# The list of steps of a hand-scheduled attention and ELU kernel is written anew

## The chip, the cores and the metric

One core of one Trainium2 chip runs the whole program. The metric is the device time of one execution in microseconds (us). TensorE (PE) multiplies matrices, its weight loads are shown as an engine of their own (PEld), VectorE (DVE), ScalarE (ACT) and GpSimd (POOL) work on elements, and SyncE (SP) issues DMAs. ACT and POOL issue DMAs as well.

## The reference, cut to what matters

```
B, H, S, D = 8, 8, 576, 64;  factor = 4;  scale = 1/8
q_d, k_d, v_d = means of q, k, v over each 4 positions          # 144 positions
out_d     = softmax(scale * q_d @ k_d.T) @ v_d                  # coarse attention
out_local = softmax(scale * q @ k.T where |i-j| < 4) @ v        # a band of 7 keys
attn = repeat(out_d, 4) + out_local                             # [8, 8, 576, 64]
x = attn.transpose(0, 2, 1, 3).reshape(4608, 512)
h = x @ w_in                                                    # [4608, 2048]
g = where(h > 0, h, exp(min(h, 0)) - 1)                         # ELU
out = g @ w_out                                                 # [4608, 512], float32
```

## The kernel before, in words

**Attention.** A batch b has eight heads, taken as four pairs j. The scores of a pair are made transposed, in six windows of 96 queries against 112 keys, beside a coarse score of 144 by 144. Exponentials are taken without a maximum, the band is cut out by a mask, the sums of the exponentials come from matmuls with an indicator (constant IND), and their reciprocals are spread over partitions: by matmuls for b = 0 to 2, by a round trip through DRAM for b = 3 to 7.

**The two large products.** The tokens go in nine blocks t of 512. For each block, 16 groups fc of 128 hidden columns are made by four matmuls each (128x128 weights, 512 columns), pass through the ELU, and are then summed by 16 steps of four matmuls into four output tiles.

**One list sets every order.** Nothing is scheduled at run time. The string ORDER holds 1524 words, and the builder walks through it once; each engine gets its instructions in the order of the words that use it and executes them strictly in that order. What crosses engines is held by semaphores alone. The words that this document uses, with b the batch, j the pair, t the token block:

- `Lq b.j`, `Lk b.j`, `Lv b.j`: a load of float32 q, k or v of one pair, issued by SyncE (lines 306 and 316). From b = 3 the loads of q and k, and all loads of v, go in runs of 256 bytes. They land in ten buffers (tag f32). `Dq b.h`, `Dk b.h` (line 336): loads that cast, issued by POOL, two pairs at a time, for b = 1 and 2. `WL`: a one-element memset on POOL that keeps the next `Lv` from starting before POOL is there. `WI`, `WO`: quarters of the two weight matrices, issued by POOL.
- `Cq`, `Ck`, `Cv`: POOL's cast to float16, which frees the load's buffer.
- `Tq`, `Tk`: transposes on PE; `Aq`, `Ak`: ACT's copy out of PSUM; `Fq`, `Fk`, `KD`: sums of four on DVE; `VS`: coarse v on PE (from b = 3 within `Tq`), `VD` its copy out on DVE.
- `SC`: the scores of a pair on PE (for b = 0 in two parts, `SL`, `SD`); `E0`, `E1`: their exponentials on ACT, two instructions each; `M`: the mask on DVE; `DEN`, `RC`: the sums on PE and the reciprocals on DVE; `RB`: the spreading matmuls; `SO`, `SI`: the round trip, issued by ACT.
- `OUT`: the product with v on PE; `LG`: ACT's copy of it out of PSUM (b = 0 to 2); `MUL`: the division on DVE; `X b.j.t`: the sum of both attentions into the token block t, on POOL.
- `Q`, `mm1.t.fc`: the first product; `e`, `m`, `g`: exponential on ACT, minimum on DVE, and sum on DVE (into tile gt); `mm2.t.i`: a quarter of an output tile; `oc`: its copy out of PSUM on ACT; `st`: its store to DRAM, issued by ACT.
- `Zn`: n matmuls on constants put before the next use of the tag "two" in PSUM; `FILL`: nine of them at the start.

**PSUM.** From the first product on there are three pools of two slots: tag "two" (all of attention's tiles: a transpose, each head of a score, a product, a spread, a coarse v take one slot each), "hp" (first product) and "misc" (output tiles, sums, some of block 0's first product). A matmul that takes a slot waits for the engine that empties the slot's last tile.

**DMA completion.** The DMAs that SyncE and ACT issue share eight completion semaphores, dealt out in the order of the list, so a store or a round trip of ACT can be given the semaphore of an earlier load of SyncE. In the built program the later DMA is not issued before the earlier one on its semaphore has landed. In the list before, `st.0.0` waits in this way for `Lv2.1`, and `st.0.1` for `Lq3.0`.

**PE's tile shapes.** A matmul uses 128x128 of the array, or a part: 64x64 (`Tq`, `Tk` for b below 3), 64x128 (`SC`), 128x64 (`OUT`), 128x32 (`DEN`), 32x128 (`RB`).

Of the kernel before, what the change touches and what calls it, by code (L numbers as in the profile page):

```python
# [29 lines left out]
RW = RG * RN  # L30
# [18 lines left out]
Tk1.0 Aq1.0 m.0.3 m.0.1 Ak1.0 g.0.1 WO3 SC1.1 Fq1.0 WLv2.0 Dq2.0 Lv2.0 mm1.0.7 Fk1.0 E01.1 Lv2.1
Cv1.0 Lv2.2 g.0.3 E11.1 Lv2.3 g.0.2 VS1.0 Lq3.0 mm1.0.11 VD1.0 e.0.7 M1.1 mm1.0.13 e.0.6 m.0.7  # L50
e.0.11 g.0.7 SC1.0 m.0.6 e.0.13 mm1.0.5 m.0.11 g.0.11 E01.0 m.0.13 mm1.0.9 E11.0 g.0.13 g.0.6
Tq1.2 Tk1.2 M1.0 Aq1.2 mm1.0.14 Ak1.2 Lk3.0 Cv1.1 Fq1.2 OUT1.0 e.0.5 Fk1.2 mm1.0.4 e.0.9 m.0.5
LG1.0 g.0.5 Tq1.3 e.0.4 Dq2.1 m.0.9 VS1.1 g.0.9 Aq1.3 mm2.0.0 VD1.1 e.0.14 Fq1.3 Tk1.3 OUT1.1
Ak1.3 Dk2.1 m.0.4 g.0.4 LG1.1 Fk1.3 SC1.2 m.0.14 g.0.14 mm2.0.1 E01.2 mm1.0.12 E11.2 mm1.0.8
e.0.12 M1.2 SC1.3 Lv3.0 m.0.12 e.0.8 g.0.12 Cv1.2 E01.3 m.0.8 mm1.0.10 g.0.8 E11.3 VS1.2 e.0.10
mm1.0.15 M1.3 VD1.2 DEN1 e.0.15 m.0.10 g.0.10 OUT1.2 m.0.15 mm2.0.2 RC1 LG1.2 g.0.15 RB1.1 RB1.0
MUL1.1 mm2.0.3 MUL1.0 X1.1.1 RB1.2 oc.0.0 MUL1.2 X1.0.2 mm2.0.4 X1.1.2 X1.0.1 Tq2.1 st.0.0 Tk2.1
Aq2.1 Cv1.3 mm2.0.5 Ak2.1 Fq2.1 X1.2.1 VS1.3 Fk2.1 Tq2.2 X1.2.2 mm2.0.6 Aq2.2 VD1.3 OUT1.3 Fq2.2
RB1.3 LG1.3 mm2.0.7 MUL1.3 Tk2.2 oc.0.1 mm2.0.8 Cv2.0 Lq3.1 Ak2.2 mm2.0.9 X1.3.2 Fk2.2 X1.3.1
mm2.0.10 st.0.1 Cv2.1 mm2.0.11 VS2.0 oc.0.2 mm2.0.12 Cv2.2 Lk3.1 VD2.0 SC2.1 mm2.0.13 E02.1  # L60
# [124 lines left out]
def kernel(  # L185
# [92 lines left out]
    def nines(b):  # L278
        return b in NINES
# [481 lines left out]
```

## Time and profile before

| what | value |
|---|---|
| median of 6 runs | 365.6 us (364.04 to 368.89) |
| the profiled execution | 365.09 us, of which the span of its instructions is 363.3 us |
| granted TensorE clock, mean | 0.995 |
| PE busy | 348.5 us, 3953 matmuls |
| of these, first product and second product | 142.8 us and 139.8 us, 576 matmuls each |
| DVE, ACT, POOL busy | 240.3, 208.3, 120.3 us |
| DMA | 46.08 MB; 92314 of 106917 packets under 512 bytes |

The span runs from the first instruction to the last; 1.8 us of the execution lie outside it. In the trace a line such as L679 is a line of the kernel before. A matmul's end is modelled, so that matmuls that run one after the other overlap a little in the rows; the starts are what one counts with. "Idle before" is the time that the engine stood still ahead of a row, with what ended it. SPq and ACTq are the queues on which SyncE and ACT issue DMAs: a row there lasts from the start of the issue to its end, not to the landing.

### The profile page before, as it was taken

How to read it: one execution, taken by the hardware profiler on the slowest of the kernel's cores; microseconds unless marked ns; L12 is line 12 of the kernel's file. 1: busy time of each engine (PE TensorE's matmuls, PEld its weight loads, DVE VectorE, ACT ScalarE, POOL GpSimd, SP SyncE). 2: the span in 40 equal slices, each digit the busy share in tenths (PEclk: the TensorE clock that was granted, in tenths of full speed). 3: DMA queues.
4: the chain of work that ended last, by engine and by line, in shares of the span. 5: the costliest groups of instructions: out<-in, count | busy, mean ns of one | idle time of the engine just before them, and what ended most of it. 6: DMA issues, size and time to landing. Idle time of an engine off the chain costs nothing.

```text
span 363.3 us, 9507 instructions
## 1 busy us (share of the span) xinstructions
PE 348.5 (96%) x3953; PEld 183.0 (50%) x3953; DVE 240.3 (66%) x472; ACT 208.3 (57%) x395; POOL 120.3 (33%) x177
## 2 busy tenths in 40 slices
PE   7888989899999999999999999999999999999995
PEld 3564455545565564564555445554544544444442
DVE  2767986459888548587887677878565655455520
ACT  2855883478578759377466666776454334344321
POOL 6858224551474140850472218311400410000000
PEclk9899999999999999999999999999999999999999
DMA  8999999999879789499469942022004100010012
GB/s 269 222 203 200 200 197 196 201 175 197 155 149 208 117 181 167 101 213 190 113 114 195 203 75 69 32 83 60 31 33 112 56 34 30 29 60 29 29 60 87
DMA packets 106917, 46.08 MB, mean 127 GB/s; under 512 B 92314, under 2 KB 101178, under 8 KB 106874
## 3 DMA queue, kind: packets, MB, share of 16 engines
q1 hardware_dynamic: 91402, 25.17, 41.0%
q10 hardware_dynamic: 8896, 13.36, 12.6%
q0 software_dynamic: 6576, 6.94, 11.1%
q8 instruction: 31, 0.51, 0.6%
q14 instruction: 12, 0.10, 0.1%
HBM read 42.49 MB, written 9.53 MB: 143 GB/s over the span
## 4 chain that ended last, share of the span: by engine, by line
PE 78%; ACT 6%; DVE 4%; DMA 4%; issue 3%; SPq 2%; ACTq 1%; POOL 1%; POOLq 0%
PE op L679 32%; PE hp L635 28%; DMA v<-in_v_dram 4%; PE sc L476 3%; PE lg L584 3%; DVE gt L669 2%; PE den L539 2%; SPq L316 2%; ACT e L660 2%; PE tq L369 1%; PE tq L392 1%; PE tk L392 1%; PE tq L251 1%; ACT pex L502 1%; DVE e L664 1%
## 5 line engine op out<-in xcount | busy, mean ns | idle before, releaser
L635 PE MATMUL hp<-xt,WI 128*128 128x512 f16 x576 | 142.8, 379 | 2.2 <-DVE gt L669 2.0
L679 PE MATMUL op<-WO,gt 128*128 128x512 f16 x576 | 139.8, 380 | 0.4 <-DVE gt L669 0.3
L660 ACT ACTIVATE e<-hp 128x512 f16<-128x512 f32 x144 | 85.7, 601 | 74.3 <-PE hp L635 67.1
L669 DVE SCALAR_TENSOR_TENSOR gt<-hp,e 128x512 f16<-128x512 f32 x144 | 99.2, 690 | 4.7
L679 PEld LDWEIGHTS <-gt 128*128 128x128 f16 x576 | 53.2, 98 | 62.0 <-DVE gt L669 1.6
L635 PEld LDWEIGHTS <-WI 128*128 128x128 f16 x576 | 53.0, 97 | 60.8 <-issue 3.7
L664 DVE TENSOR_SCALAR e<-e 128x512 f16<-128x512 f16 x144 | 51.9, 362 | 47.9 <-ACT e L660 47.0
L627 POOL TENSOR_TENSOR xt<-ln,gn 128x64 f16<-128x64 f16 (+7 forms) x63 | 41.7, 684 | 66.8 <-DVE ln L614 66.4
L502 ACT ACTIVATE pex<-sc 112x576 f16<-112x576 f32 x64 | 40.9, 646 | 6.6 <-PE sc L486 4.2
L686 ACT COPY os<-op 128x512 f32<-128x512 f32 x36 | 21.1, 586 | 40.1 <-PE op L679 39.9
L359 POOL CAST v<-v 112x768 f16<-112x768 f32 x30 | 24.9, 842 | 37.2 <-PE lg L584 22.6
L521 DVE TENSOR_TENSOR mex<-pex,MASK 112x1152 f16<-112x1152 f16 x32 | 25.5, 797 | 13.2 <-ACT pex L502 13.1
L354 POOL CAST q<-q 96x768 f16<-96x768 f32 x20 | 16.8, 840 | 31.1 <-issue 21.3
L354 POOL CAST k<-k 96x768 f16<-96x768 f32 x20 | 17.3, 873 | 27.2 <-PE tk L392 20.6
L508 ACT ACTIVATE dex<-sc 72x288 f16<-72x288 f32 x64 | 25.4, 403 | 0.9 <-PE sc L486 0.9
L417 ACT CAST qt<-tq 128x720 f16<-128x720 f32 x20 | 15.2, 760 | 11.4 <-PE tq L369 7.9
L476 PEld LDWEIGHTS <-kt 64*112 64x112 f16 x384 | 13.3, 129 | 14.0 <-issue 10.1
L476 PE MATMUL sc<-qt,kt 64*112 64x96 f16 x384 | 17.2, 220 | 2.1 <-ACT kt L412 0.6
L369 PEld LDWEIGHTS <-VR 112*72 112x72 f16 x192 | 13.3, 115 | 5.8 <-ACT qt L412 2.2
L614 DVE TENSOR_TENSOR ln<-lg,rcb 128x576 f16<-128x576 f32 x20 | 15.0, 749 | 0.0
L450 DVE CAST vd<-tq 72x256 f16<-72x256 f32 x20 | 8.3, 414 | 8.8 <-ACT qt L417 8.7
L584 PEld LDWEIGHTS <-v 112*64 112x64 f16 x384 | 10.2, 109 | 7.4 <-issue 5.3
(64 smaller groups left out, 273.7 us busy)
## 6 DMA issues: line engine op xcount, KB each, us to landing
v<-in_v_dram SPq DMA_DIRECT2D x28, 336.0 KB, 7.5
out_dram<-os ACTq DMA_DIRECT2D x36, 256.0 KB, 2.8
q<-in_q_dram SPq DMA_DIRECT2D x24, 288.0 KB, 5.2
k<-in_k_dram SPq DMA_DIRECT2D x24, 288.0 KB, 6.1
rcb<-rd ACTq DMA_DIRECT2D x10, 360.0 KB, 5.4
WI<-in_moe_w_in_dram POOLq DMA_DIRECT2D x4, 512.0 KB, 11.6
WO<-in_moe_w_out_dram POOLq DMA_DIRECT2D x4, 512.0 KB, 16.4
q<-in_q_dram POOLq DMA_DIRECT2D x4, 288.0 KB, 11.5
```

The lines of the kernel that those rows point to most:

```text
L354: nc.gpsimd.tensor_copy(out=t, in_=x.rearrange("p (e c d) -> p c e d", e=2, d=D))
L359: nc.gpsimd.tensor_copy(out=t[:], in_=st32.pop(("v", b, j)).rearrange("p (e c) d -> p c e d", e=2))
L476: nc.tensor.matmul(sc[e][0:KW, c // 3, QB * (c % 3) : QB * (c % 3) + QB], kt[r, QB * c : QB * c + KW], q_of(b, j, r, c), start=True, stop= ...
L502: nc.scalar.activation(out=stS[(b, j)][2][:, e, :].rearrange("p (g u) -> p g u", g=2), in_=scs[(b, j)][e][0:KW, :, 0:HB], func=AF.Exp, sca ...
L508: nc.scalar.activation(out=stS[(b, j)][1][:, e], in_=scs[(b, j)][e][0:KG, :, HB : HB + SD], func=AF.Exp, scale=SCALE / 16.0,)
L521: nc.vector.tensor_tensor(out=mex[:], in0=pex[:], in1=mk2, op=AB.mult)
L627: eng.tensor_tensor(out=xts[t][:, j, t0 - TBLK * t : t1 - TBLK * t], in0=ln[:, a:z], in1=_rep4(gn[:, a // 4 : z // 4]), op=AB.add,)
L635: nc.tensor.matmul(hps[(t, fc)][:], WI[:, dc, 128 * fc : 128 * fc + 128], xts[t][:, dc, :], start=(dc == 0), stop=(dc == DMC - 1),)
L660: nc.scalar.activation(out=e[:], in_=hps[(t, fc)][:], func=AF.Exp)
L664: nc.vector.tensor_scalar(out=e[:], in0=e[:], scalar1=1.0, scalar2=-1.0, op0=AB.min, op1=AB.add)
L669: nc.vector.scalar_tensor_tensor(out=gts[t][:, fc, :], in0=hps[(t, fc)][:], scalar=0.0, op0=AB.max, in1=els.pop((t, fc))[:], op1=AB.add,)
L679: nc.tensor.matmul(ops[(t, tt)][:], gts[t][:, fc, 128 * tt : 128 * tt + 128], WO[:, fc, :], start=(fc == 0), stop=(fc == FCN - 1),)
```

## The change

The list is replaced. The new one holds the same 1524 words, each once more, in another order; the first 29 us of PE's work (to `Q2`) keep PE's, ACT's and DVE's order, and the order of SyncE's loads is the same throughout. Three things in the code go with it:

- the tile of `LG` (tag lg32) becomes one tile of twice the width for each two pairs, two buffers instead of four, so `LG` of pair 0 must come before that of pair 1, and 2 before 3;
- IND has 104 columns instead of 52 (the built load moves 112x104 instead of 112x52 elements);
- `load_v4`, `V4` and `STORE_SP` are added and not used: V4 is empty and STORE_SP is False, and no word of the list calls `U` or `V`.

From `X0.2.1` to `X1.3.1` (about 28 to 70 us of the profile before) the two lists read as follows.

```
-X0.2.1 X0.2.0 Q1 X0.3.0 Dk1.1 Q2 Dq1.1 mm1.0.0 mm1.0.2 e.0.0 X0.3.1 Tq1.1 WO0 Tk1.1 e.0.2 m.0.0
-mm1.0.1 g.0.0 Ak1.1 WO1 mm1.0.3 Aq1.1 m.0.2 mm1.0.6 Fk1.1 WO2 e.0.3 Fq1.1 e.0.1 Tq1.0 Dk2.0
-Tk1.0 Aq1.0 m.0.3 m.0.1 Ak1.0 g.0.1 WO3 SC1.1 Fq1.0 WLv2.0 Dq2.0 Lv2.0 mm1.0.7 Fk1.0 E01.1 Lv2.1
-Cv1.0 Lv2.2 g.0.3 E11.1 Lv2.3 g.0.2 VS1.0 Lq3.0 mm1.0.11 VD1.0 e.0.7 M1.1 mm1.0.13 e.0.6 m.0.7
-e.0.11 g.0.7 SC1.0 m.0.6 e.0.13 mm1.0.5 m.0.11 g.0.11 E01.0 m.0.13 mm1.0.9 E11.0 g.0.13 g.0.6
-Tq1.2 Tk1.2 M1.0 Aq1.2 mm1.0.14 Ak1.2 Lk3.0 Cv1.1 Fq1.2 OUT1.0 e.0.5 Fk1.2 mm1.0.4 e.0.9 m.0.5
-LG1.0 g.0.5 Tq1.3 e.0.4 Dq2.1 m.0.9 VS1.1 g.0.9 Aq1.3 mm2.0.0 VD1.1 e.0.14 Fq1.3 Tk1.3 OUT1.1
-Ak1.3 Dk2.1 m.0.4 g.0.4 LG1.1 Fk1.3 SC1.2 m.0.14 g.0.14 mm2.0.1 E01.2 mm1.0.12 E11.2 mm1.0.8
-e.0.12 M1.2 SC1.3 Lv3.0 m.0.12 e.0.8 g.0.12 Cv1.2 E01.3 m.0.8 mm1.0.10 g.0.8 E11.3 VS1.2 e.0.10
-mm1.0.15 M1.3 VD1.2 DEN1 e.0.15 m.0.10 g.0.10 OUT1.2 m.0.15 mm2.0.2 RC1 LG1.2 g.0.15 RB1.1 RB1.0
-MUL1.1 mm2.0.3 MUL1.0 X1.1.1 RB1.2 oc.0.0 MUL1.2 X1.0.2 mm2.0.4 X1.1.2 X1.0.1 Tq2.1 st.0.0 Tk2.1
-Aq2.1 Cv1.3 mm2.0.5 Ak2.1 Fq2.1 X1.2.1 VS1.3 Fk2.1 Tq2.2 X1.2.2 mm2.0.6 Aq2.2 VD1.3 OUT1.3 Fq2.2
-RB1.3 LG1.3 mm2.0.7 MUL1.3 Tk2.2 oc.0.1 mm2.0.8 Cv2.0 Lq3.1 Ak2.2 mm2.0.9 X1.3.2 Fk2.2 X1.3.1
-mm2.0.10 st.0.1 Cv2.1 mm2.0.11 VS2.0 oc.0.2 mm2.0.12 Cv2.2 Lk3.1 VD2.0 SC2.1 mm2.0.13 E02.1
...
+X0.2.1 X0.2.0 Q1 X0.3.0 X0.3.1 Dk1.1 Q2 Dq1.1 mm1.0.0 Tq1.1 e.0.0 mm1.0.2 WO0 Aq1.1 Tk1.1 m.0.0
+mm1.0.1 g.0.0 WO1 e.0.2 mm1.0.3 Tq1.0 Ak1.1 Fq1.1 Dk2.0 mm1.0.6 Aq1.0 m.0.2 Fk1.1 WO2 e.0.3
+Tk1.0 e.0.6 Fq1.0 Lv1.3 Cv1.0 Ak1.0 g.0.2 WO3 VS1.0 m.0.6 e.0.1 mm1.0.8 g.0.6 WLv2.0 Dq2.1 VD1.0
+mm1.0.4 m.0.1 g.0.1 SC1.1 Fk1.0 mm1.0.7 E01.1 m.0.3 g.0.3 E11.1 mm1.0.9 e.0.4 M1.1 SC1.0 e.0.7
+m.0.4 e.0.8 g.0.4 E01.0 m.0.8 g.0.8 e.0.9 Tq1.3 m.0.7 E11.0 mm1.0.10 m.0.9 g.0.9 Dq2.0 Aq1.3
+Tq1.2 M1.0 Lv2.0 mm1.0.13 Aq1.2 Fq1.3 Cv1.1 Tk1.2 Fq1.2 VS1.1 Ak1.2 g.0.7 Tk1.3 Fk1.2 e.0.10
+mm1.0.11 Dk2.1 VD1.1 Ak1.3 m.0.10 e.0.13 OUT1.0 g.0.10 e.0.11 mm1.0.5 Fk1.3 LG1.0 m.0.11
+mm1.0.15 g.0.11 e.0.5 m.0.13 SC1.2 g.0.13 mm2.0.0 E01.2 m.0.5 g.0.5 mm1.0.12 e.0.15 E11.2 m.0.15
+mm2.0.1 g.0.15 e.0.12 M1.2 SC1.3 Lv2.1 mm1.0.14 m.0.12 E01.3 g.0.12 Cv1.2 E11.3 OUT1.1 mm2.0.2
+e.0.14 M1.3 LG1.1 m.0.14 VS1.2 g.0.14 DEN1 VD1.2 OUT1.2 RC1 LG1.2 RB1.2 mm2.0.3 MUL1.2 RB1.1
+oc.0.0 X1.2.1 RB1.0 st.0.0 mm2.0.4 MUL1.0 X1.2.2 mm2.0.5 MUL1.1 X1.0.2 X1.0.1 mm2.0.6 Lv2.2
+X1.1.1 Tq2.1 Tk2.1 Aq2.1 Cv1.3 mm2.0.7 Ak2.1 Fq2.1 X1.1.2 Tq2.2 oc.0.1 Fk2.1 VS1.3 Aq2.2 mm2.0.8
+VD1.3 st.0.1 Fq2.2 OUT1.3 RB1.3 Cv2.0 Lv2.3 LG1.3 mm2.0.9 MUL1.3 Tk2.2 mm2.0.10 Ak2.2 X1.3.2
+X1.3.1 Fk2.2 VS2.0 Lq3.0 Tq2.0 VD2.0 Cv2.1 mm2.0.11 Aq2.0 Fq2.0 mm2.0.12 oc.0.2 Cv2.2 Lk3.0
```

The rest of the code:

```
 X_DVE, K_DVE = ((0, 3, 0),), ((0, 0), (0, 1))
+V4, STORE_SP = (), False
...
@@ -157,9 +158,10 @@
     vr = np.zeros((KW, 120), dtype=np.float16)
     for i in range(QB):
         vr[PAD + i, 48 + i // 4] = 0.25
-    ind = np.zeros((KW, 52), dtype=np.float16)
+    ind = np.zeros((KW, 104), dtype=np.float16)
     ind[:, 19] = 1.0
     ind[:, 39:51] = 1.0
+    ind[:, 52:104] = 4.0 * ind[:, 0:52]
     sel = np.zeros((NPAIR, 32, RN, 2, 64), dtype=np.float16)
     for e in range(2):
         for g in range(RN):
@@ -270,7 +272,7 @@
         src = moe_w_out.rearrange("(c p) m -> p c m", p=128)[:, n, :]
         nc.gpsimd.dma_start(out=WO[:, n, :], in_=src)
 
-    st32, st16, stV, stT, stS, stR = {}, {}, {}, {}, {}, {}
+    st32, st16, stV, stT, stS, stR, st4 = {}, {}, {}, {}, {}, {}, {}
     tp, scs, dens, rbs, lgs, lg32, lns, rcbs = {}, {}, {}, {}, {}, {}, {}, {}
     xts, gts, ops, hps, els, oss = {}, {}, {}, {}, {}, {}
     kts = {}
@@ -342,6 +344,25 @@
         )
         for i in range(2):
             st16[(n, b, 2 * h + i)] = t[:, i]
+
+    def wide():
+        return sb.tile([128, 2 * RW], FP32, tag="lg32", bufs=2, name="lg32")
+
+    def load_v4(h, b, i):
+        if not h:
+            t = wide()[0:KG, 0:1024].rearrange("p (g h d) -> p g h d", h=2, d=D)
+            for n in range(2):
+                st4[(b, 2 * i + n)] = t[:, 4 * n : 4 * n + 4]
+            st4[(b, i, "all")] = t
+        a = v[b, 4 * i]
+        nc.gpsimd.dma_start(
+            out=st4[(b, i, "all")],
+            in_=bass.AP(
+                tensor=a.tensor, offset=a.offset + 2 * D * h,
+                ap=[[4 * D, KG], [4 * D * KG, 8], [D, 2], [1, D]],
+            ),
+            **({"accum_op": AB.add} if h else {}),
+        )
 
     def cast_qk(n, b, j):
         t = sb.tile([128, 768], FP16, tag=n + "16", bufs=2, name=n + "16")
@@ -393,7 +414,7 @@
                 to[:, c // 3, QW * (c % 3) : QW * (c % 3) + QW], x[:, c, :, :],
                 at_once("I16")[:], start=True, stop=True,
             )
-        if n == "q":
+        if n == "q" and b not in V4:
             vsum_mm(b, j, to[:, :, GW : GW + 128])
 
     def away(n, b, j):
@@ -445,6 +466,12 @@
         vsum_mm(b, j, x)
 
     def v_away(b, j):
+        if b in V4:
+            vd = sb.tile([KG, 4, D], FP16, tag="vd", bufs=7, name="vd")
+            x = st4.pop((b, j))
+            nc.vector.tensor_tensor(out=vd[:], in0=x[:, :, 0], in1=x[:, :, 1], op=AB.add)
+            stV[(b, j)][1] = vd
+            return
         x = tp[("v", b, j)] if nines(b) else tp[("q", b, j)][:, :, GW : GW + 128]
         vd = sb.tile([KG, 2, 128], FP16, tag="vd", bufs=7, name="vd")
         nc.vector.tensor_copy(out=vd[:], in_=x[0:KG])
@@ -527,7 +554,8 @@
         for e in range(2):
             for g in range(RN):
                 r = RN * e + g
-                st = at_once("IND")[:, 19 - r : 51 - r]
+                o = 52 if b in V4 and g >= 8 else 0
+                st = at_once("IND")[:, o + 19 - r : o + 51 - r]
                 for kg in range(1 if g < 8 else 2):
                     for j in range(NPAIR):
                         mex, dex, _ = stS[(b, j)]
@@ -589,13 +617,15 @@
             for e in range(2):
                 nc.tensor.matmul(
                     lg[64 * e : 64 * e + 64, 0, HB : HB + SD],
-                    vd[:, kg, 64 * e : 64 * e + 64], dex[:, e, kg, :],
+                    vd[:, 2 * e + kg] if b in V4 else vd[:, kg, 64 * e : 64 * e + 64], dex[:, e, kg, :],
                     start=(kg == 0), stop=(kg == 1),
                 )
 
     def out_away(b, j):
         lg = lgs[(b, j)]
-        t = lg32[(b, j)] = sb.tile([128, RW], FP32, tag="lg32", bufs=4, name="lg32")
+        if j % 2 == 0:
+            lg32[(b, j // 2, 0)] = wide()
+        t = lg32[(b, j)] = lg32[(b, j // 2, 0)][:, RW * (j % 2) : RW * (j % 2) + RW]
         nc.scalar.copy(
             out=t[:, 0:S].rearrange("p (g u) -> p g u", g=2), in_=lg[:, :, 0:HB]
         )
@@ -687,7 +717,8 @@
 
     def store(t, tt):
         r = TBLK * t + 128 * tt
-        nc.scalar.dma_start(out=out[r : r + 128, :], in_=oss.pop((t, tt))[:])
+        eng = nc.sync if STORE_SP else nc.scalar
+        eng.dma_start(out=out[r : r + 128, :], in_=oss.pop((t, tt))[:])
 
     def first_fill():
         tp[("q", 0, 0)] = two("tq")
@@ -711,6 +742,8 @@
         does["T" + n] = lambda b, j, n=n: turn(n, b, j)
         does["A" + n] = lambda b, j, n=n: away(n, b, j)
         does["F" + n] = lambda b, j, n=n: fours(n, b, j)
+    does["U"] = lambda b, j: load_v4(0, b, j)
+    does["V"] = lambda b, j: load_v4(1, b, j)
     for i in range(2):
         does[f"E{i}"] = lambda b, j, i=i: exp_both(i, b, j)
         does[f"G{i}"] = lambda b, j, i=i: exp_local(i, b, j)
```

## The prediction

> **What bounds the kernel now.** I read the page's busy shares first, then PE's slices.
>
> ```profile
> PE 348.5 (96%) x3953; PEld 183.0 (50%) x3953; DVE 240.3 (66%) x472; ACT 208.3 (57%) x395; POOL 120.3 (33%) x177
> ...
> PE   7888989899999999999999999999999999999995
> ...
> ACT  2855883478578759377466666776454334344321
> ```
>
> PE is the bound, and as the same 3953 matmuls run in any order, a new list can win only the holes between them. The first eight slices (9 us each) hold most of the holes, so I cut the span by stage.
>
> ```profile
> core 0: us, PE busy (x) PEld busy (x) DVE busy (x) ACT busy (x) POOL busy (x), PEclk, DMA share, GB/s
> 0.00:27.90 27.90, 23.50 (x458) 14.66 (x459) 15.69 (x26) 15.15 (x31) 18.81 (x38) 0.94 1.11 230
> 27.90:64.50 36.60, 31.86 (x526) 17.22 (x524) 28.52 (x58) 23.61 (x49) 16.22 (x25) 1.00 1.20 198
> 64.50:95.00 30.50, 29.62 (x452) 16.25 (x453) 20.98 (x40) 20.55 (x41) 9.74 (x13) 1.00 1.17 193
> 95.00:300.00 205.00, 203.99 (x2249) 108.51 (x2248) 148.51 (x294) 126.34 (x238) 75.54 (x102) 1.00 0.58 115
> 300.00:359.70 59.70, 59.54 (x274) 26.38 (x272) 26.56 (x56) 22.08 (x39) 0.00 (x0) 1.00 0.12 45
> ```
>
> Columns: stretch, its length, busy time of each engine, granted clock. The DMA engines are full to 95 us. I then laid the list's words on the PE rows, start to start, and took for each kind of block its shortest distance as its work. Work is 339.0 us; 22.8 us are lost: about 9 before `mm1.0.0` at 30.49, 4.2 from there to 62, 2.0 in one hole at 62 to 65, 3.8 from 65 on, 3.8 behind PE's last block. The rest of the hole's story is in the chain that ended last.
>
> ```profile
> 49.02 14.32 DMA v<-in_v_dram
> ...
> 63.42 0.38 ACTq L690
> ...
> 63.84 0.65 ACT qt L412
> ...
> 64.53 0.53 PE vs L369 x6
> ```
>
> `Lv2.1` was 14.3 us under way. The store `st.0.0` could not be issued before (shared completion semaphore), so ACT stood; `Aq2.1` behind it came at 63.84, `VS1.3` (which needs its slot) at 64.53 instead of 62.66: 1.87 us.
>
> **The change part by part.** Every duration is from this one execution, 365.09 us (span 363.3 and 1.8 outside); it lies 0.5 under the median, so I sum against 365.09 and shift the result by 0.5.
>
> *To `mm1.0.0`:* PE, ACT and DVE keep their order. POOL swaps `WI` and `Dk1.0`, `Dq1.0`, all issues of some 0.75 us, with consumers far behind. Nothing; without that cover, one issue's 0.75 us. IND doubles to 22.8 KB of a 46 MB program: nothing. The paired lg32 buffers cost nothing, as DVE's `MUL` of one batch ends long before `LG` of the next; uncovered, `LG` waits one division, 0.75 us.
>
> *30.49 to `VS1.3`.* I stepped the new list through with these rows: a group of four matmuls 0.863 us (0.957 before another tile shape), `SC` 0.566, `OUT` 0.505, `e` 0.55 start to start on ACT, an exponential pair 0.83, an ACT copy 0.52, `m` 0.36, `g` 0.69, a cast 0.84 and an issue 0.75 on POOL. Two resources give waits: ACT behind exponentials and POOL behind issues. One in full: from the start of `SC1.1` PE needs 0.566 + 0.863 + 0.957 + 0.72 (a wait of `mm1.0.9` for `g.0.3`) + 0.566 = 3.67 us to `Tq1.3`, which takes the slot that `E01.0` empties. ACT starts 0.73 + 0.07 after `SC1.1`, does two pairs (1.66), `e.0.4`, `e.0.7`, `e.0.8` (1.64), then `E01.0` (0.83), ready at 4.95: a wait of 1.3. Queued behind the waiting `Tq1.3` is all of PE. The others, found so: `VS1.0` 0.9 (its cast stands behind POOL's issues, as it did before with 1.0), `mm1.0.8` 0.44, `mm1.0.9` 0.72, `RB1.2` 0.35 (reciprocals), `VS1.1` 0.25, `Tk1.3`, `OUT1.1` 0.17 each, `mm1.0.4` 0.1. Sum 4.45 against 4.19 before (0.55, 0.49, 0.49, 1.01, 0.14, 0.30, 0.68, 0.38, 0.15): **+0.3**.
>
> The row for such waits in the kernel before:
>
> ```profile
> 34.85 0.20 PE L476 MATMUL sc<-qt,kt 64*112 64x96 f16 x1 [0.45 <-ACT qt L412]
> 35.39 0.46 PE L476 MATMUL sc<-qt,kt 64*112 64x96 f16 x11 [0.34 <-ACT kt L412]
> ...
> 37.78 0.49 PE L369 MATMUL vs<-v,VR 112*72 112x128 f16 x6 [0.83 <-ACT dex L508]
> ```
>
> The last is named for ACT; POOL's cast of that v ended at 37.72, and it is what ended the wait.
>
> *The store wait.* SyncE's loads keep their order and, under full DMA engines, I let them land as before: `Lv2.1` 63.35, `Lq3.0` 69.08 (issued 61.96).
>
> ```profile
> v<-in_v_dram SPq DMA_DIRECT2D x1, 336.0 KB, 14.3
> ...
> q<-in_q_dram SPq DMA_DIRECT2D x1, 288.0 KB, 7.1
> ```
>
> In the new list three more quarters of `mm2` lie ahead of `Tq2.1`, so PE comes there at about 63.9 and `st.0.0` holds nobody. But `st.0.1`, tied to `Lq3.0`, is moved forward past `LG1.3` (before, it stood at `mm2.0.10`, issued 69.16 with nothing urgent behind). ACT now stands at it until 69.1; 0.38 for the issue and 0.81 for `LG1.3` end at 70.4, and `Tk2.2` waits for that slot. PE's work up to `Tk2.2` is 55.64 us in the new list; with 8.94 lost before `mm1.0.0` and 4.45 since, PE would be there at 69.0. The wait is 1.4, against 1.87 + 0.11 that disappear: **−0.6**. The stall is moved, not removed. Behind it on ACT are `Ak2.2`, `Aq2.0`, the first `e.1`. Unknown is the landing: by the two rows above the load takes 7.1 or 14.3 us; I take 7.1, the row of the same load. At the page's median for q, 5.2, it lands at 67.2 and costs nothing.
>
> The Trainium skill, page "DMA: Bandwidth & Descriptors", section "Anatomy of one DMA — SWDGE (gpsimd) path", fits a load's time as 2.0 us plus its bytes at 436 GB/s, for loads that POOL issues. That speaks against my wait: by it 288 KB are an estimated 2.7 us, `Lq3.0` lands near 64.7, and the sum would be 1.4 lower. The rows of 7.1 and 14.3 us for loads on SyncE's queue decide; this case does not show such speed while the queue is full.
>
> *Changes of tile shape.* Counted in built order PE changes shape 172 times before and 175 after.
>
> ```profile
> 141.60 1.89 PE L635 MATMUL hp<-xt,WI 128*128 128x512 f16 x8
> 143.42 0.51 PE L476 MATMUL sc<-qt,kt 64*112 64x96 f16 x12
> ```
>
> Eight matmuls at 0.216 are 1.73; the score starts 1.82 after: 0.09 for the change. Three more: **+0.3**.
>
> *65 us to the end.* Before, ten waits make 3.3 of the 3.8 us, nearly all for `g` (an hp slot is needed again too soon).
>
> ```profile
> L635 PE MATMUL hp<-xt,WI 128*128 128x512 f16 x576 | 142.8, 379 | 2.2 <-DVE gt L669 2.0
> L679 PE MATMUL op<-WO,gt 128*128 128x512 f16 x576 | 139.8, 380 | 0.4 <-DVE gt L669 0.3
> ```
>
> By the rows a slot comes free some 1.9 us after its last matmul (`e`, `g` in sequence); a gap of 1.52 filled with other PE work gave 0.38. In the new list such gaps are wide enough at `mm1.2.11`, `mm2.2.2`, `mm1.3.11`, `mm1.4.5`, `mm1.8.3`, `mm2.8.3` (0.38, 0.38, 0.31, 0.25, 0.18, 0.43): −1.9. New tight ones are `mm1.1.3` (gap 1.52: 0.4), `mm1.2.9` (1.75: 0.15), `VS2.1` (0.23) and `RB2.0` (0.1): +0.9. **−1.0**. Bounds: all 3.8 but the 0.9 and a last 0.2 go, −2.7; nothing is gained and the denser ACT work at 90 to 120 us (27 us of work in 30 instead of 23) costs 1.5, +1.5. I take −1.0, nearest to the counted gaps.
>
> Sum: 0 + 0.3 − 0.6 + 0.3 − 1.0 = −1.0. 365.09 becomes 364.1, the median **364.6**. It is no change that can be measured: 1%, 3.7 us, is about what a measurement of this kernel tells from none.
>
> **The rivals.**
>
> R1, faster. `Lq3.0` lands by 67.8 (the median of 5.2 us for q speaks for it, full DMA engines against), `st.0.1` costs nothing, and the 2.8 us of later waits vanish too, as the large holes past 65 us are few. 364.6 − 1.3 − 2.8 = 360.5.
>
> R2, slower. `st.0.1` is moved ahead of `LG1.3` and its load is late like `Lv2.1`: 14.3 us from 61.96 is 76.3, 7.2 later than 69.08, and ACT with PE behind it stands so much longer: 364.6 + 7.2 = 371.8. It decides, slower by over 1% (369.3), from a landing at 73.8 on. For it: loads of v before it took that long, and POOL's issues of WO and the casting loads compete on the same engines. Against: the loads issued from 56 to 66 us took 6 to 9 us.
>
> R3, the change does not do what it says: 172 shape changes become 175 and SyncE's order is the same, so a count of shapes wins nothing, and only those 0.3 us remain: 365.9.
>
> **How the numbers follow.** Forecast 0.55, R1 0.20, R2 0.20, R3 0.05. Faster by over 1% (under 361.9) is R1 and a little of the forecast, 0.21; slower is R2 and 0.04 of the forecast, 0.24; the rest 0.55. The range goes from R1's 360.5 to 370.5: what is left out is half of R2 and the end of R1. The forecast's own range is its two open terms, −1.3 (load) − 1.7 (later waits) to +2.5 (later waits): 361.6 to 367.1.
>
> **What would show it.** Right: no hole at 62, a wait of ACT of more than 1 us ended by a q load at 67 to 70, `Tk2.2` near 70.4, a 1.3 us wait at `Tq1.3` near 42, under 3 us of PE waits past 71, 3.8 us at the end. Wrong: an ACT wait at `st.0.1` past 73 or none; PE waits of several us for casts between 33 and 60; new waits for `g` past 90 us that sum to over 4.

## The result, and the profile after

| | before | after |
|---|---|---|
| median of the runs measured together | 366.44 us (70 runs) | 370.68 us (33 runs, 365.83 to 373.44) |
| ratio | | 1.0076, interval 1.0056 to 1.0096 |
| the profiled execution, and its span | 365.09, 363.3 us | 369.86, 368.1 us |
| mean granted clock over the span of the profiled execution | 0.995 | 0.986 |
| PE lost, as the prediction counts it: before `mm1.0.0` / to `Tk2.2` / to the last block | 8.9 / 6.1 / 3.9 us | 10.2 / 8.3 / 4.9 us |

It is slower, by 0.8%; 1.0 us less was forecast. The ratio is smaller than that of the medians (1.0116) because the comparison leaves out the runs that lie more than 1.5% above a kernel's fastest, which for the changed kernel are ten runs with a low granted clock; where the fastest of few runs was itself short of the full clock (e3 and e4 below), none is left out.

First four of the five stretches that were shown before the change: length, busy time of each engine, granted clock, DMA share. From 300 us on PE does not stand.

```profile
core 0: us, PE busy (x) PEld busy (x) DVE busy (x) ACT busy (x) POOL busy (x), PEclk, DMA share, GB/s
0.00:27.90 27.90, 23.04 (x442) 14.26 (x443) 14.76 (x24) 14.66 (x30) 17.60 (x36) 0.94 1.11 230
27.90:64.50 36.60, 31.51 (x477) 17.16 (x475) 27.99 (x53) 22.26 (x48) 12.97 (x20) 0.91 1.20 200
64.50:95.00 30.50, 29.80 (x383) 15.84 (x383) 20.49 (x39) 19.05 (x40) 15.04 (x20) 1.00 1.08 205
95.00:300.00 205.00, 202.85 (x2371) 109.15 (x2366) 149.29 (x297) 127.62 (x239) 75.05 (x102) 1.00 0.55 112
```

From 27.9 to 64.5 us PE is about as busy as before (31.5 against 31.9 us) but does 49 matmuls fewer, and the granted clock is 0.91 where it was 1.00. That column had no term in the prediction. From 95 to 300 us PE stands 1.1 us longer. PE's waits, by what ended them (total, times, longest):

```profile
PE vs L390 <- POOL v L380: 2.6, 1, 2.6
PE tq L407 <- ACT dex L535: 1.7, 1, 1.7
...
PE sc L503 <- DVE vd L477: 0.9, 1, 0.9
...
PE op L709 <- DVE gt L699: 0.7, 1, 0.7
```

The first two stand in the first product of block 0. They are `VS1.0` and `Tq1.3` on PE's timeline:

```profile
35.11 0.47 PE L407 MATMUL tk<-EYE,k 64*64 64x64 f16 x18
38.23 0.80 PE L390 MATMUL vs<-v,VR 112*72 112x128 f16 x6 [2.65 <-POOL v L380]
38.82 3.05 PE L665 MATMUL hp<-xt,WI 128*128 128x512 f16 x8
41.80 0.51 PE L503 MATMUL sc<-qt,kt 64*112 64x96 f16 x12
...
46.58 0.47 PE L407 MATMUL tq<-EYE,q 64*64 64x64 f16 x18 [1.70 <-ACT dex L535]
```

Eight matmuls of the first product take 1.82 us elsewhere, from their start to that of the score behind them; behind the first hole they take 2.98 (38.82 to 41.80). POOL's timeline tells why `VS1.0` is so late:

```profile
35.89 0.70 POOL L338 DMA_DIRECT2D k<-in_k_dram  x1 [1.61 <-PE tk L407]
36.58 0.77 POOL L273 DMA_DIRECT2D WO<-in_moe_w_out_dram  x1
37.34 0.84 POOL L380 CAST v<-held 112x768 f16<-112x768 f32 x1
```

`Dk2.0` reuses a buffer that `Tk1.0` reads, so POOL stands until PE has done `Tk1.0`; then come two issues and the cast `Cv1.0`, 2.3 us in a row. The new list has `VS1.0` on PE right behind `Tk1.0`, so all of that chain is PE's wait. Before, `SC1.1` and `mm1.0.7` stood between: 1.4 us of work and a wait of 0.5.

The clock is best read on its own grid. Cut into pieces of 3.41 us that begin where its steps are:

```profile
34.32:37.74 3.42, 1.26 (x22) 0.66 (x21) 3.38 (x7) 2.75 (x6) 1.85 (x3) 1.00 1.30 198
37.74:41.15 3.41, 2.92 (x12) 1.47 (x12) 2.51 (x6) 0.00 (x0) 1.83 (x4) 0.50 1.21 197
41.15:44.56 3.41, 3.41 (x40) 1.63 (x39) 1.40 (x3) 2.10 (x5) 0.00 (x0) 1.00 1.22 198
44.56:47.98 3.42, 1.72 (x36) 0.95 (x34) 3.20 (x9) 3.42 (x9) 0.00 (x0) 1.00 1.21 198
47.98:51.39 3.41, 3.41 (x45) 1.90 (x45) 2.76 (x5) 1.24 (x3) 1.55 (x2) 0.50 1.21 195
```

A piece in which PE worked 37% (1.26 of 3.42) or 50% of the time is followed by a whole piece at half clock. All slow stretches of all profiles here, ahead of PE's last block, last one, two or three times 3.41 us and lie on one grid in each execution; where the grid starts differs from execution to execution. The Trainium skill, page "TensorE: Matmul & The Clock Gate", section "Part 1: The HAM clock gate (the "warmup" mystery)", describes this: a free-running window of 3.4 us over which PE's activity is measured. It states a fall to half after an idle window; here a half-busy one was enough.

### The profile page after: what moved, and what is told of

Read it like the earlier page. It is cut to its first block, busy times and chain, and to the rows that moved or that the text cites. A ratio compares the mean times of both kernels' runs of the same rounds, so it can differ in the third digit from the quotient of the medians.

```text
span 368.1 us, 9501 instructions
## 1 busy us (share of the span) xinstructions
PE 351.6 (96%) x3953; PEld 185.4 (50%) x3953; DVE 241.3 (66%) x472; ACT 208.5 (57%) x395; POOL 120.7 (33%) x177
## 4 chain that ended last, share of the span: by engine, by line
PE 85%; ACT 5%; DVE 5%; issue 2%; DMA 1%; POOL 1%; SPq 0%; ACTq 0%
PE op L709 33%; PE hp L665 32%; PE sc L503 4%; PE lg L612 3%; DVE e L694 2%; PE den L567 2%; PE tq L390 2%; ACT pex L529 2%; PE tq L413 1%; PE tk L413 1%; DVE gt L699 1%; DMA k<-in_k_dram 1%; PE rb L601 1%; ACT e L690 1%; PE vs L390 1%
## 5 line engine op out<-in xcount | busy, mean ns | idle before, releaser
L665 PE MATMUL hp<-xt,WI 128*128 128x512 f16 x576 | 144.3, 384 | 0.7 <-DVE gt L699 0.6
L694 DVE TENSOR_SCALAR e<-e 128x512 f16<-128x512 f16 x144 | 53.3, 370 | 58.5 <-ACT e L690 57.7
L380 POOL CAST v<-v 112x768 f16<-112x768 f32 x30 | 25.2, 848 | 11.9 <-PE lg L612 10.2
L503 PEld LDWEIGHTS <-kt 64*112 64x112 f16 x384 | 13.2, 129 | 13.7 <-issue 10.4
L441 ACT CAST kt<-tk 128x576 f16<-128x576 f32 x20 | 12.9, 643 | 2.5 <-PE tk L413 1.7
```

The lines of the kernel that those rows point to most:

```text
L380: nc.gpsimd.tensor_copy(out=t[:], in_=st32.pop(("v", b, j)).rearrange("p (e c) d -> p c e d", e=2))
L503: nc.tensor.matmul(sc[e][0:KW, c // 3, QB * (c % 3) : QB * (c % 3) + QB], kt[r, QB * c : QB * c + KW], q_of(b, j, r, c), start=True, stop= ...
L665: nc.tensor.matmul(hps[(t, fc)][:], WI[:, dc, 128 * fc : 128 * fc + 128], xts[t][:, dc, :], start=(dc == 0), stop=(dc == DMC - 1),)
L694: nc.vector.tensor_scalar(out=e[:], in0=e[:], scalar1=1.0, scalar2=-1.0, op0=AB.min, op1=AB.add)
```

## The experiments

Each kernel is one of the two lists with some words moved. "Middle" is what PE loses from `mm1.0.0` to `Tk2.2` and "late" from there to its last block, both from the one profiled execution; the clock is the mean over all runs of that kernel, 6 to 12 of each experiment. Matmuls on constants count as lost. The kernel before ran beside each: medians 365.8 to 367.0, clock 0.989 to 0.991 in each set.

| run | median us | ratio to before, interval | clock | middle | late |
|---|---|---|---|---|---|
| changed kernel | 370.7 | 1.0076 (1.0056 to 1.0096) | 0.984 | 8.3 | 4.9 |
| e1_cast_early | 368.6 | 1.0056 (1.0024 to 1.0088) | 0.988 | 4.0 | 5.4 |
| e2_fill | 370.4 | 1.0094 (1.0056 to 1.0133) | 0.985 | 6.0 | 5.3 |
| e3_vs_early | 370.6 | 1.0116 (1.0068 to 1.0164) | 0.980 | 9.1 | 3.6 |
| e4_ind52 | 372.2 | 1.0141 (1.0086 to 1.0196) | 0.980 | 7.6 | 4.9 |
| e5_both | 370.3 | 1.0091 (1.0058 to 1.0125) | 0.984 | 6.3 | 4.9 |
| e6_both_x | 371.7 | 1.0124 (1.0077 to 1.0171) | 0.984 | 10.5 | 7.5 |
| e7_store | 365.3 | 0.9987 (0.9959 to 1.0015) | 0.991 | 4.5 | 3.7 |
| e8_hybrid | 369.9 | 1.0093 (1.0058 to 1.0128) | 0.986 | 6.8 | 3.9 |
| e9_before_newstart | 365.9 | 0.9977 (0.9946 to 1.0008) | 0.990 | 6.1 | 3.5 |
| e10_after_oldstart | 370.3 | 1.0084 (1.0057 to 1.0112) | 0.984 | 7.6 | 4.9 |
| e11_e1_oldstart | 367.7 | 1.0030 (1.0004 to 1.0056) | 0.990 | 4.2 | 5.4 |
| e12_three_parts | 367.2 | 1.0010 (0.9980 to 1.0039) | 0.991 | 5.7 | 3.8 |
| e13_hole_filled | 366.9 | 1.0000 (0.9970 to 1.0031) | 0.994 | 7.5 | 3.8 |
| e14_before_cast_early | 366.0 | 0.9985 (0.9957 to 1.0014) | 0.990 | 5.2 | 3.7 |
| e15_best | 366.9 | 0.9989 (0.9958 to 1.0020) | 0.990 | 4.2 | 4.4 |

**The hole at `VS1.0`, and the clock behind it.** First the cast alone:

```
-... Ak1.1 Fq1.1 Dk2.0 mm1.0.6 Aq1.0 m.0.2 Fk1.1 WO2 e.0.3 Tk1.0 e.0.6 Fq1.0 Lv1.3 Cv1.0 Ak1.0
+... Ak1.1 Fq1.1 Lv1.3 Cv1.0 Dk2.0 mm1.0.6 Aq1.0 m.0.2 Fk1.1 WO2 e.0.3 Tk1.0 e.0.6 Fq1.0 Ak1.0
```

> The changed list with Cv1.0 moved ahead of Dk2.0 on POOL, all else as it was. Theory W (the place of VS1.0 costs the time: PE stands behind Tk1.0 for POOL's chain Dk2.0, WO2, Cv1.0): the idle time before VS1.0 falls from 2.65 us to under 0.5 and the granted clock stays 1.0 from 36 to 42 us; 2.3 us of wait and 1.4 us of slow clock go, so the time falls by 3 to 4 us and is 0.2 to 0.5% under or level with the kernel before. Rival S (what is saved here is lost again at the store st.0.1, which waits for Lq3.0 at 68 to 69 us): the wait goes, but under 1 us is left of it at the end. Rival P (the loss is in the prologue's constants and the rest of the code): no change from the changed kernel, 0.7% over the kernel before.

The wait at `VS1.0` is gone and no piece of the middle is at 0.5: the middle loses 4.0 us where it lost 8.3. The median falls 2.1 us where theory W expected 3 to 4, and the kernel is still 0.6% over the kernel before; the intervals of the two ratios overlap. The waits at `st.0.1` (rival S) did not come. Then matmuls on constants in the hole instead:

```
-... Ak1.0 g.0.2 WO3 VS1.0 m.0.6
+... Ak1.0 g.0.2 WO3 Z9 VS1.0 m.0.6
```

> The changed list with nine matmuls on constants (Z9, 1.94 us) ahead of VS1.0; POOL's chain and the end of PE's wait stay where they are. If the granted clock falls because PE stands idle, it now stays at 1.0 from 38 to 42 us: VS1.0 still starts near 38.2 and the time falls by about 1.4 us against the changed kernel, 0.3 to 0.4% over the kernel before. If the clock has another cause or costs nothing, 0.50 in the same place and the time of the changed kernel, 0.7 to 1.1% over.

In the profile the clock stays at 1.0 from 20 us on and the middle loses 2.3 us less. But the median and the mean clock of the twelve runs are those of the changed kernel: a miss. The 1.8 us hole at `Tq1.3` is still there. In the profiled execution the grid cut it so that its emptiest piece (from 40.56 us) has PE busy 2.18 of 3.41 us; a piece laid from 41.05 would have 1.71, half. In the profile of e12 (below), which has a hole there too, of 1.3 us, a piece with PE busy 1.82 us is followed by a slow one. So the hole that was left can cost the clock where the grid lies otherwise; whether it did in the other eleven executions isn't seen, as only one is profiled. The reverse, the hole put into the kernel before:

```
-SC1.1 Fq1.0 WLv2.0 Dq2.0 Lv2.0 mm1.0.7 Fk1.0 E01.1 Lv2.1 Cv1.0 Lv2.2 g.0.3 E11.1 Lv2.3 g.0.2 VS1.0
+Fq1.0 WLv2.0 Dq2.0 Lv2.0 Fk1.0 Lv2.1 Cv1.0 Lv2.2 VS1.0 SC1.1 mm1.0.7 E01.1 g.0.3 E11.1 Lv2.3 g.0.2
```

> The kernel before with VS1.0 ahead of SC1.1 and mm1.0.7 on PE (POOL's order kept), so that PE stands for Cv1.0 right behind Tk1.0, from 34.3 to 37.8 us, 3.4 us in place of 1.0 + 0.5. Theory W: 1.9 us more wait, a granted clock of 0.5 for some 3 us behind it that costs another 1.4; 2 to 4 us slower, +0.5 to +1.0%; part of it may be hidden as the store st.0.0 frees PE at 64.5 whatever came before, by up to 1.9 us. Theory S taken alone (the store's load at 63.4 sets VS1.3 in the kernel before): under 1 us slower.

It is 1.2% slower, 4 us, a little over theory W. PE stands 3.4 us, and two pieces of the clock's grid go to half:

```profile
36.49:39.91 3.42, 0.55 (x36) 0.54 (x29) 3.39 (x8) 1.47 (x3) 2.57 (x5) 1.00 1.22 201
39.91:43.32 3.41, 2.65 (x24) 1.69 (x24) 0.95 (x2) 0.62 (x2) 1.28 (x2) 0.50 1.24 204
43.32:46.73 3.41, 3.41 (x9) 1.21 (x8) 1.94 (x4) 2.74 (x7) 0.00 (x0) 0.50 1.21 196
```

To tell the hole's length from the clock behind it, the same list as e3 with `Z13` ahead of `VS1.0`:

> The kernel before with VS1.0 ahead of SC1.1 and mm1.0.7, as in the third run, and thirteen matmuls on constants (2.8 us) ahead of it, so that PE works through most of the 3.4 us that it stands there; the wait ends when Cv1.0 ends, as in that run. If a hole costs the clock behind it on top of its length: no stretch at 0.5 from 38 to 47 us and 1.5 to 3 us faster than that run (which was 1.2% over the kernel before), so 0.4 to 0.8% over. If the clock behind the hole is not what costs: 1.0 to 1.3% over, as that run.

```profile
34.63 0.45 PE L382 MATMUL tk<-EYE,k 64*64 64x64 f16 x18
35.53 2.97 PE L247 MATMUL vs<-busy 128*128 128x512 f16 x13 [0.45 <-ACT qt L408]
38.46 0.49 PE L365 MATMUL vs<-v,VR 112*72 112x128 f16 x6
```

The two pieces behind the hole's start, which happen to lie on the same grid as in e3, now are at full clock:

```profile
36.49:39.91 3.42, 3.08 (x32) 1.67 (x29) 2.41 (x5) 0.00 (x0) 1.92 (x4) 1.00 1.21 196
39.91:43.32 3.41, 3.40 (x34) 1.63 (x29) 1.67 (x4) 3.23 (x7) 0.00 (x0) 1.00 1.22 196
```

PE comes to `SC1.1` hardly earlier (7.7 us behind `mm1.0.0`, 8.0 in e3), yet the kernel is back at 1.000, better than expected, and its mean clock is the highest of all, 0.994. So in the place where this hole stands its length costs next to nothing (the hole of the kernel before at `VS1.3`, 1.9 us there, is 0.3 us here, and takes most of it up), and the clock behind it costs the 4 us. This settles it for this hole: idle time was replaced by useless work, and the time came back; the two intervals lie apart. For the two holes of the changed kernel it is not settled in this way, as e2 brought nothing.

**The constant.** The width of IND goes back to 52:

```
-    ind = np.zeros((KW, 104), dtype=np.float16)
+    ind = np.zeros((KW, 52), dtype=np.float16)
...
-    ind[:, 52:104] = 4.0 * ind[:, 0:52]
```

> The changed kernel with IND 52 columns wide as before. Theory W: no change, within 0.2% of the changed kernel (0.6 to 1.0% over the kernel before). Theory P (the doubled constant delays the first load, which landed at 4.75 us in place of 4.30, and all behind it): 0.7 us or more faster than the changed kernel, with the first product at 30.5 in place of 31.8 us.

Theory P falls: it is not faster. At 1.4% over the kernel before it lies above what theory W gave too. Five of its six runs had a clock of 0.976 to 0.980; the sixth, at 0.994, took 368.3 us. By the intervals it can't be told from the changed kernel.

**Both waits, DVE and POOL, the store, the joint.** In e5 the exponentials for `Tq1.3` come earlier as well:

```
-SC1.0 e.0.7 m.0.4 e.0.8 g.0.4 E01.0 m.0.8 g.0.8 e.0.9 Tq1.3 m.0.7 E11.0 mm1.0.10
+SC1.0 E01.0 m.0.4 e.0.8 g.0.4 E11.0 m.0.8 g.0.8 e.0.7 Tq1.3 m.0.7 e.0.9 mm1.0.10
```

> The changed list with both large early waits taken away: Cv1.0 ahead of Dk2.0 as in the run before, and E01.0 and E11.0 ahead of e.0.8, e.0.7 and e.0.9 on ACT, so that Tq1.3 gets its slot earlier. Theory C (PE's idle stretches in the first product of block 0 cost their own length and let the granted clock fall to 0.5 in the 3 to 4 us behind them): the waits at VS1.0 (2.7) and Tq1.3 (1.8) shrink to under 1 us together, no stretch at 0.5 lies between 36 and 60 us, the mean granted clock of the runs comes back to that of the kernel before (0.990, against 0.984 of the changed kernel); 4 to 6 us under the changed kernel: 364 to 366 us, 0 to 0.5% under the kernel before. Rival S (the store st.0.1, whose load lands at 68 to 69 us, takes the place of the waits): PE stands over 1 us at Tk2.2 near 69 us, and the time is 367 or more.

A miss. `Tq1.3` still waits 1.1 us, and the `e` pushed back make new waits for `g`: 1.1 us each ahead of `mm1.0.8`, `mm1.0.5` and `mm1.0.15`. The wait was moved to the hp slots. The clock stays at 0.984, though no hole in the middle is over 1.2 us. Two things in its trace bear on that. The slow stretch of the profiled execution (22.9 to 33.2 us) lies ahead of the words that tell e5 from e1. And the waits ahead of `mm1.0.5` and `mm1.0.15` are 2 us apart; the emptiest piece of the execution's own grid there has PE busy 69%, but a piece laid 1 us later would hold both, with PE busy 43%:

```profile
51.30:54.71 3.41, 1.46 (x21) 0.74 (x18) 3.38 (x8) 1.39 (x4) 0.75 (x1) 1.00 1.21 198
```

Such a piece could cost the clock in executions with that grid; none of them was profiled, so the low clock of e5 stays open. e6 is e5 with three of POOL's sums on DVE:

```
-X_DVE, K_DVE = ((0, 3, 0),), ((0, 0), (0, 1))
+X_DVE, K_DVE = ((0, 3, 0), (2, 3, 3), (5, 2, 6), (5, 3, 5)), ((0, 0), (0, 1))
```

> As e5_both, and three of POOL's sums (X2.3.3, X5.2.6, X5.3.5) go to DVE. Theory L (the waits past 100 us come from a minimum m on DVE that is held up while POOL works through several instructions in a row: 2.13 us for m.4.9 and 1.6 for m.1.12, where 0.27 is usual without POOL): m.4.9 under 0.9 us, the wait of mm2.4.3 (0.9) gone, 1 to 1.5 us under e5_both. Rival (the late waits come from the order alone, or POOL's casts hold DVE up just as long): the wait at mm2.4.3 stays over 0.5, no gain, or 0.5 us more by DVE's added work.

A miss with a lesson. In the changed kernel DVE's minimum `m.4.9` took 2.22 us (0.29 for its neighbours) while POOL had a cast and sums in a row:

```profile
222.81 0.29 DVE L694 TENSOR_SCALAR e<-e 128x512 f16<-128x512 f16 x1
...
225.50 2.22 DVE L694 TENSOR_SCALAR e<-e 128x512 f16<-128x512 f16 x1
```

```profile
225.95 0.81 POOL L380 CAST v<-v 112x768 f16<-112x768 f32 x1
226.73 2.17 POOL L657 TENSOR_TENSOR xt<-ln,gn 128x384 f16<-128x384 f16 x3
```

In e6 the sum that was given to DVE at the same place was itself held up, 2.48 us, by the sums left on POOL, and `mm2.4.3` waited 2.5 us instead of 0.9:

```profile
225.51 2.48 DVE L653 TENSOR_TENSOR xt<-ln,gn 128x384 f16<-128x384 f16 x1
```

Behind that wait came a slow piece too, 188 us after the last one before it:

```profile
226.36:229.77 3.41, 1.59 (x22) 1.13 (x20) 3.38 (x5) 1.90 (x4) 3.30 (x5) 1.00 0.21 77
229.77:233.18 3.41, 3.41 (x9) 1.22 (x8) 1.48 (x5) 0.49 (x1) 1.70 (x2) 0.50 0.44 100
```

Both traces fit the reading that DVE stands for POOL; no run took POOL's work away at that place, so it is not shown by itself. The cure was wrong. e7 is the kernel before with the store out of the way:

```
-X1.0.1 Tq2.1 st.0.0 Tk2.1 Aq2.1 Cv1.3 mm2.0.5 Ak2.1 Fq2.1
+X1.0.1 Tq2.1 Tk2.1 Aq2.1 Cv1.3 mm2.0.5 Ak2.1 st.0.0 Fq2.1
```

> The kernel before with st.0.0 moved behind Aq2.1, Ak2.1 in the list, so that ACT does not stand at the store ahead of the copies that PE waits for. By the reading of the hole at 62 us: the wait of 1.87 us at VS1.3 goes and up to 0.2 us of new waits come; 1.5 to 1.9 us faster, 0.4 to 0.5%. Rival (what stands behind, Tq2.2 and the casts of v, waits as long): under 0.5 us.

The hole at `VS1.3` shrinks from 1.87 to 0.33 us as read, but the time moves by no more than the interval. A reading that fits: the hole ended at a fixed time, the landing of `Lv2.1` at 63.4 us, so it took up whatever was late before it; the start of e7's execution was 1.5 us later than that of the one profiled before. e8 joins e5's list up to `Fk2.2` to the rest of the kernel before:

> The list of e5_both up to Fk2.2 (about 70 us), behind it the remaining words in the order of the kernel before, in the code of before. The waits from Tk2.2 to the last block are 3.9 us by the trace of before and 4.9 to 5.4 by those of the changed list: 1.0 to 1.5 us under e5_both if the late order of the changed list is the worse one; no change or slower if the joint between the two orders costs more than 1 us.

The late waits come down to 3.9 us as expected; the ratio doesn't show it (1.0093 against 1.0091). The intervals are 0.7% wide, so 1 us would not be seen in them, and the rival isn't excluded.

**Which part of the list.** e9 and e10 exchange the words up to `mm1.0.0`, e11 does it for e1's list, e12 is the start of before, the middle of e1 and the late part of before.

> The kernel before with the words up to mm1.0.0 in the order of the changed list (POOL's casts, issues and sums move, PE, ACT and DVE keep their order), the rest of its own list. Theory Q (the start of the changed list, by what POOL does when, makes the start longer or the clock fall oftener): 1.0 to 2.5 us slower than the kernel before. Theory R (the start is the same but for chance; what is lost is lost behind 30 us): within 0.5 us of the kernel before.

> The changed kernel with the words up to mm1.0.0 in the order of the kernel before. Theory Q: 1.0 to 2.5 us faster than the changed kernel (0.1 to 0.5% over the kernel before). Theory R: as the changed kernel, 0.8 to 1.2% over the kernel before.

> The changed list with Cv1.0 ahead of Dk2.0, and the words up to mm1.0.0 in the order of the kernel before. The waits from mm1.0.0 to Tk2.2 were 4.0 us in the first run with that cast moved, against 6.2 in the kernel before, and those from there to the end 5.4 against 3.9. Theory Q: the start is as in the kernel before, so the time is 0 to 1 us under it. Theory R: as the first run with the cast moved, 1.5 to 2.5 us over the kernel before.

> Start of the kernel before, the changed list with the cast moved from mm1.0.0 to Fk2.2, and the remaining words in the order of the kernel before (in its code). By the sums of waits, start as before, 4.0 against 6.2 in the middle and 3.5 to 3.9 at the end, 1.5 to 2.5 us under the kernel before if the start decides (theory Q); by theory R 1 to 2 us over it.

The start is innocent within the intervals (theory R): with the new one the kernel before stays at 0.998, with the old one the changed kernel stays at 1.008. With the cast moved as well it is 1.003, which lies between the two theories, and with the late part of before 1.001, under what theory R gave. Most of the difference between the lists is thus in the middle. The one cast is worth 0.5% from e10 to e11 but 0.2% from the changed kernel to e1 (2.6 and 2.1 us of the medians), the late part perhaps 0.2% (e11 against e12, intervals overlap).

**A version that might beat both.** e14 moves only `Cv1.0` ahead of `Dk2.0` in the kernel before; e15 does that, e7's move of the store and e9's start.

> The kernel before with Cv1.0 ahead of Dk2.0 on POOL and nothing else. The wait of VS1.0 (1.0 us at 36.8) goes; the hole at 62 to 64.5 us ends with the load of v whatever comes before it, so it grows by what is saved: under 0.3 us faster. If waits ahead of that hole count in full: 1.0 us faster.

> The kernel before with its start in the changed list's order, Cv1.0 ahead of Dk2.0 and st.0.0 behind Ak2.1. The waits of 1.0 us at VS1.0 and of 1.9 us at VS1.3 go both: 2 to 3 us faster than the kernel before, 0.5 to 0.8%, if what comes behind (the load Lq3.0 at st.0.1, Cv1.3 for VS1.3) is not late in their place; else 0.2 to 0.4%.

e14 is 0.15% faster, 0.5 us, with an interval from 1.6 us faster to 0.5 slower, which doesn't tell its two theories apart. e15 misses: PE's middle loses 4.2 us against 6.1, both waits are down to 0.2 and 0.3, and yet the time is that of the kernel before. Its profiled start took 10.5 us of losses against 8.9; in the profiles of all kernels here that figure goes from 8.0 to 13.2 with hardly any change in the instructions, more than any step of the list is worth. No version beat the kernel before by more than its interval.

## Why the prediction was wrong, by its own steps

Two steps failed: the clock, which had no term, and the last, from 65 us to the end. Two more were off and cancelled.

**The start: nothing.** Right within the intervals of e9 and e10. The 1.3 us by which the profiled execution was later there is chance: with the old start `mm1.0.0` came at 30.5 to 33.6 us in eight profiles, with the new one at 29.6 to 34.8 in nine.

**30.49 to `VS1.3`: +0.3.** At full clock the new list lost 5.8 us there (8.3 less 2.5 for the slow pieces; behind `VS1.3` hardly anything), against 4.2 before: +1.6. Its listed terms add up to 4.40, not 4.45. `VS1.0` was put at 0.9 and took 2.7: POOL's issues and cast were counted, but not that `Dk2.0`, ahead of them, cannot start before `Tk1.0` ends on PE, so that nothing in front of PE can hide them. `Tq1.3` was put at 1.3 and took 1.8: `E01.0` freed its slot 4.8 us after `SC1.1`, near the 4.95 of the sum, but the 0.72 that `mm1.0.9` was to wait ahead of it did not come. The waits at `mm1.0.8` and `mm1.0.4` did not appear either, since PE was late by then.

**The clock: not in the sum at all.** This is the first step that failed. Every duration was taken at a clock of 1.0 because the page of before showed 1.00 from 27.9 us on. A hole of 2.7 us and one of 1.8 were priced at their length; the slow pieces behind them added 2.5 us in the profiled execution (1.4 after the first, 1.1 after the second). The runs give a share as well. At a mean clock of 0.999 or 1.000, the kernel before took 364.2 to 364.5 us (7 runs) and the changed kernel 365.8 to 366.2 (3 runs): 1.6 us more without any slow piece. The means of all runs with a clock on record are 366.5 (110 runs) and 370.2 (34). So of 3.7 us, about 2.1 come with the clock and 1.6 do not.

**The store wait: −0.6.** The hole at `VS1.3` went, as forecast, but not by moving to `Tk2.2`: `Lq3.0` landed at 68.3 (69.08 forecast), and `st.0.1` was issued at 71.3, when PE and ACT had come late enough for other reasons. The 1.4 us at `Tk2.2` never came, so the term was −1.9. That this and the +1.6 above make the forecast −0.3 together is luck. Two quarters of `mm2`, not three, were added ahead of `Tq2.1`. R2's load was not late, so R2 is not what made it slower.

**Changes of shape: +0.3.** Not tested by itself.

**65 us to the end: −1.0, measured +1.0.** This is the second step that failed. The six waits that were to go went (1.9 us), and so did 0.84 at `mm1.1.4`, which had not been counted; `mm1.1.3` and `VS2.1` came at 0.38 and 0.23 as priced. Not foreseen: `SC3.0` 0.97, `mm2.4.3` 0.91, `VS2.2` 0.50, `mm1.2.6` 0.46, and four of 0.2 to 0.25. The first two follow long minima on DVE while POOL ran: `m.1.12` took 1.67 us and `m.4.9` 2.22, where the median is 0.29. The step took 0.36 for `m`, the mean. It is not one execution's chance: with the new late order the profiles lose 4.9 to 5.4 us late (e6, which changed DVE's work, 7.5), with the old one 3.5 to 4.4.

**The sum.** Waits at full clock, the late part and shapes make −0.3 + 1.0 + 0.3 = +1.0 in the profiled execution, where the runs at full clock show 1.6; with 2.1 for the clock it is 3.7 between the means (4.2 between the medians). What is open is which holes cost the clock in which executions: filling or shortening them helped in e1, e11 and e13 and not in e2 and e5.

## What to carry to other kernels

Price an idle stretch of PE by the clock behind it, not by its length alone: one of 3.4 us, with 6.8 us at half clock behind it, cost 4 us in a place where its own length cost next to nothing. When a consumer is moved next to the instruction that starts its producer's chain, follow that chain through every engine; a queue counted as busy may be one that waits for you. And ahead of a wait that ends at a fixed time, such as a load's landing, nothing that is saved counts, by the reading of e7 and e13.

## What the runs showed of the hardware

- The granted clock went to 0.50 in steps of 3.41 us. Between 30 and 70 us, every piece of the grid with PE busy 53% or less was followed by a slow one (16, 22, 23, 37, 47, 50 and 53%), and no full-speed piece at 62 to 66% was; in the start, with its small matmuls, pieces at 75 to 82% went both ways, and slow pieces with PE busy 91 to 100% were followed by another slow one. So the busy share of the profile is not all that decides. Three executions of the changed kernel had a mean clock of 0.999; none of them was profiled, so what its holes were there isn't known.
- An execution's mean clock comes in levels near 1.000, 0.995, 0.990, 0.986, 0.981 and 0.976, one for each slow piece more (3.41 us at half of 363). The spread of the changed kernel's runs is mostly that count: it took 365.8 to 366.2 us at 0.999, and 372.2 to 373.4 at 0.975 to 0.977. A line of time against the clock lost (span times 1 minus clock) has 0.76 us for each us there, but 0.45 in the kernel before (110 runs), with much scatter: what a slow piece costs is not the same in both.
- While POOL ran instructions back to back, a 16-bit minimum on DVE took 2.22 us (median 0.29) and a 16-bit sum 2.48. The Trainium skill, page "SBUF — State Buffer", section "🔬 SBUF: two separate sides", has a port pair that GpSimd locks for a whole instruction, as some DVE operations do, those with two SBUF inputs among them. If that is the cause, DVE lost it here over several POOL instructions in a row; no run here shows the lock itself.
